# A Fourier layer and a feed-forward layer on one core: where the feed-forward's streamed operands lie, relative to its weights, modulo 512 bytes

## The chip, the core and the metric

The kernel runs on one core of a Trainium2 chip. The core has a matrix engine (PE, TensorE), whose matmuls take a *stationary* operand (the weights, loaded into the array by an own weight-load instruction, PEld) and a *moving* operand (streamed past them column by column), two elementwise engines that also read the matrix engine's result memory (DVE, ACT), a slower one that does not (POOL), and SP, which here only issues transfers (DMA). Operands of matmuls are read from the on-chip memory SBUF, in which each of 128 partitions has its own row of bytes; a tile's *place* below is its byte address in that row. The metric is device microseconds of one execution.

## The reference

```python
X = np.fft.rfft(x, axis=1)                      # x: 8 batches x 3008 x 256
Yr = Xr @ w_r - Xi @ w_i + b_r
Yi = Xr @ w_i + Xi @ w_r + b_i
Y = softshrink(Yr, 0.01) + 1j * softshrink(Yi, 0.01)
y = np.fft.irfft(Y, n=3008, axis=1)             # 24064 tokens of 256
h = y @ w_in                                    # 256 x 2048
out = (h * np.cos(h)) @ w_out                   # 2048 x 256
```

## The kernel before

The Fourier part is done as small matrix products in stages: stage A (along 47, line 364), stage B (forward along 64 at line 396, the mixing products at lines 420 to 422, the inverse along 64 at line 460), stage C (the last inverse, line 715), with scratch in DRAM between them. The feed-forward part works on tiles of 512 tokens (the sixth and last of a batch has 448) and on 16 slices of 128 of the 2048 hidden units. Each operand that needs more than the fast format holds is split into a high and a low part; one step of the feed-forward (`moe_step`, one tile and one slice) therefore issues six matmuls into `ph` (lines 772, 773, 774, twice: high weights by high tokens, high by low, low by high), then ACT and DVE form `h*cos(h)`, and three steps later `second` issues six matmuls into `po` (lines 742, 743 and 748, twice). Twelve matmuls a step, 96 steps a batch: 1152 a batch, of which 960 have 512 columns and 192 have 448.

The order is written by hand: the feed-forward of batch b runs on PE, and between its matmuls (`pull`) pieces of the Fourier stages of batches b+1 and b+2 are put in by a budget. Batch 7 has no such work beside it but its own stage C. Before the feed-forward of batch 0 there is a prologue of some 96 us with the Fourier stages of batch 0 and part of batch 1's.

What the change touches:

- `tokens` allocates the two tiles `xTh` and `xTl` (moving operands of lines 772 to 774), three buffers each; `moe_step` allocates `gh` and `gl` (moving operands of lines 742, 743 and 748), four buffers each. The stationary operands are 128-column (512-byte) slices of `win` (lines 772 to 774) and `wout` (742 to 748).
- Every one of those tiles is a whole number of 512 bytes long, and in the program built from the kernel `win`, `wout`, `wf`, the `wk` pool and the `mo` pool (all Fourier work tiles, `xTh`, `xTl`, `gh`, `gl`) begin at 320 modulo 512. So each feed-forward matmul has moving operand and weights at a distance of 0 modulo 512. The tiles `fa`, `fas`, `ident` and `inv`, which come ahead of `last` (1128 bytes) and `sig` (48 bytes), begin at 128 modulo 512; `inv` is the stationary operand of line 460 and `fas` that of line 364, whose moving operands (`yh`, `yl`, `xh`) begin at 320. Those two lines are at a distance of 192.
- `AO_BUFS`, the buffers of `stage_out` (tag `ao`): results of stage A (lines 326 and 366) and of the inverse of stage B (lines 463, 530 and 537), copied from the result memory by ACT and then stored to DRAM by SP's queue. The tag `xl` holds `wq`, scratch of the weight splitting (line 216).

Of the kernel before, what the change touches and what calls it, by code (L numbers as in the profile page):

```python
# [12 lines left out]
F32 = mybir.dt.float32  # L13
F32R = mybir.dt.float32r
# [13 lines left out]
NTT = 6  # L28
SKEW = 3
XP_BUFS = 5  # L30
XT_BUFS, AO_BUFS, XH_BUFS = 5, 4, 3
EARLY_W = 6
TAIL_W = 2
W_ORDER = (0, 1, 2, 3, 8, 9, 10, 11, 4, 5, 12, 6, 7, 13, 14, 15)
# [6 lines left out]
GAP = 5  # L41
A_EVERY, A_DVE = 2, 4
NP = 12
SPREAD, SPREAD_FIRST = 1.2, 1.1


# [6 lines left out]
def _split(a):  # L53
    hi = _r11(a)
    return hi, _r11(a - hi.astype(np.float64))
# [7 lines left out]
def _constants():  # L63
# [39 lines left out]
    inv = inv.reshape(2, 128, 2, 32, 2).transpose(1, 0, 3, 2, 4).reshape(128, 2, 128)  # L103
    sg = sign.reshape(64, NP, 2).transpose(2, 0, 1).reshape(128, NP)
    fh, fl = _split(fa.reshape(2, 48, -1)[0, :, :96].reshape(48, 48, 2)[:, :, 0])
# [8 lines left out]
def tile_body(ctx: ExitStack, tc, x, x2, w_r, w_i, b_r, b_i, w_in, w_out,  # L114
# [4 lines left out]
    cp = ctx.enter_context(tc.tile_pool(name="cp", bufs=1))  # L119
    wk = ctx.enter_context(tc.tile_pool(name="wk", bufs=2))  # L120
    pool = {}
    dr = ctx.enter_context(tc.tile_pool(name="dr", bufs=2, space=bass.MemoryType.DRAM))
    ps = ctx.enter_context(tc.tile_pool(name="ps", bufs=1, space=PS))

    fa = cp.tile([96, 128], F32, name="fa")
    nc.sync.dma_start(fa, c_fa)
    fas = cp.tile([112, 128], F32R, name="fas")
    ident = cp.tile([128, 128], F32, name="ident")
    inv = cp.tile([128, 2, 2, 128], F32R, name="inv")
    last = cp.tile([120, 2, 141], F32, name="last")  # L130
    sig = cp.tile([128, NP], F32, name="sig")
    bias = cp.tile([128, 2, 256], F32, name="bias")

    def load_bias():
# [15 lines left out]
    def rest(lo, x, hi):  # L150
        return nc.vector.tensor_tensor(out=lo, in0=x, in1=hi.bitcast(F32), op=ALU.subtract)  # L151
# [25 lines left out]
    def split_f64(k):  # L177

        hi, lo, _ = piece(W_ORDER[k])
        pair = raws[k].rearrange("p (n t) -> p n t", t=2)  # L180
        v, ve = pair[:, :, 1], nc.vector
        first = k < EARLY_W + TAIL_W
        m = wk.tile([128, 512], F32, tag="xh", name="wm", bufs=XH_BUFS)
        tag, bufs = (("fb", 2) if k < EARLY_W + 1 else ("z", 2)) if EARLY_W - 1 <= k and first else ("xh", XH_BUFS)

        def rest_of_words():
            low = wk.tile([128, 512], F32, tag=tag, name="wl", bufs=bufs)
            nc.scalar.activation(low, pair[:, :, 0], AF.Copy, scale=2.0 ** -52)
            return low

        def clip(engine, c):
            engine.tensor_scalar(out=c, in0=m, scalar1=F64_TINY, scalar2=F64_HUGE, op0=ALU.max, op1=ALU.min)
            return c

        def bits(c):
            ve.tensor_scalar(out=au, in0=c.bitcast(U32), scalar1=0x07FFFFFF, scalar2=3,
                             op0=ALU.bitwise_and, op1=ALU.logical_shift_left)
            ve.scalar_tensor_tensor(out=au, in0=v, scalar=0xC0000000, in1=au,
                                    op0=ALU.bitwise_and, op1=ALU.bitwise_or)

        nc.scalar.activation(m, v.bitcast(F32), AF.Abs)
        low = rest_of_words() if not first or tag != "xh" else None
        yield
        if first:
            c = clip(nc.gpsimd, m)
            yield
        bank = f"o{k % 2}" if first else "f"
        a = ps.tile([128, 512], F32, tag=bank, name="wa", bufs=1 if first else 3)
        au = a.bitcast(U32)
        bits(c if first else clip(ve, a))  # L210
        yield
        nc.scalar.copy(hi, a)
        if low is None:
            low = rest_of_words()
        yield
        q = wk.tile([128, 512], F32, tag="xl", name="wq", bufs=XH_BUFS)
        r = wk.tile([128, 512], F32, tag="cl" if k == EARLY_W + TAIL_W - 1 else "wa", name="wr", bufs=1)
        ve.tensor_scalar(out=q.bitcast(U32), in0=au, scalar1=0xFF800000, scalar2=None, op0=ALU.bitwise_and)
        rest(r, a, hi)
        yield  # L220
        nc.gpsimd.tensor_tensor(out=q, in0=low, in1=q, op=ALU.mult)
        mark["words"] = nc.gpsimd.tensor_tensor(out=lo, in0=r, in1=q, op=ALU.add)

    def piece(k):
        if k < 8:
            q, c = divmod(k, 2)
            cs = slice(512 * q, 512 * q + 512)
            return win[:, 0, c, cs], win[:, 1, c, cs], w_in[128 * c:128 * c + 128, 1024 * q:1024 * q + 1024]
        f = 2 * (k - 8)
        return tuple(wo[0][:, h, f:f + 2].rearrange("p f e -> p (f e)") for h in range(2)) + (  # L230
            w_out[128 * f:128 * f + 256, :].rearrange("(f p) e -> p f e", p=128),)
# [7 lines left out]
    def moe_w():  # L239
        for k in range(EARLY_W + TAIL_W, 16):  # L240
            steps = split_f64(k)
            with tc.issue_after(mark["gh"].ins):
                next(steps)
            yield
            for i, _ in enumerate(steps):
                if i == 0:
                    load_piece()
                yield
            yield
# [121 lines left out]
    def stage_b(b):  # L371
# [4 lines left out]
        def load(m):  # L376
            if m >= NP:
                return
            if m % 2 == 0:
                fb[m // 2] = wk.tile([128, 4, 128], F32, tag="fb", name="fb", bufs=2)  # L380
                with tc.issue_after(mark["words"].ins) if b == 1 and m < 4 else ExitStack():
                    nc.gpsimd.dma_start(fb[m // 2], c_fb[:, 2 * m:2 * m + 4])
            at[m] = stage_in("at")
            nc.sync.dma_start(at[m].rearrange("p (k d) -> p k d", k=2),
                              scr1[b][2 * m:2 * m + 2].rearrange("k r n d -> (r n) k d"))
# [83 lines left out]
        yield 2.5  # L469
        for m in range(NP + 2):  # L470
            if m < NP:
                load(m + 2)
                yield from fwd(m)
            if 1 <= m <= NP:
                yield from wmix(m - 1)
# [4 lines left out]
    def stage_b0():  # L480
# [75 lines left out]
        def words(k):  # L556

            if 0 <= k < EARLY_W + TAIL_W:
                if k not in w:
                    w[k] = split_f64(k)  # L560
                next(w[k], None)
# [119 lines left out]

    xT = {}

    def tokens(b, t):
        if (b, t) not in xT:
            xT[b, t] = tuple(pool["mo"].tile([128, 2, 512], F32R, tag=n, name=n, bufs=3) for n in ("xTh", "xTl"))
        return xT[b, t]

    def stage_c(b, t):
# [75 lines left out]
    def moe_step(b, t, f, pull):  # L765
        th, tl = xT[b, t]
        n = 512 if t < NTT - 1 else 448
        ph = ps.tile([128, 512], F32, tag="h", name="ph", bufs=3)
        h = ph[:, :n]
        fs = slice(128 * f, 128 * f + 128)  # L770
        for c in range(2):
            mm(h, win[:, 0, c, fs], th[:, c, :n], start=c == 0, stop=False)  # L772
            mm(h, win[:, 0, c, fs], tl[:, c, :n], start=False, stop=False)  # L773
            mark["ph"] = mm(h, win[:, 1, c, fs], th[:, c, :n], start=False, stop=c == 1)  # L774
        u = pool["mo"].tile([128, 512], F32, tag="u", name="u", bufs=4)
        k = u.bitcast(I32)
        gh = pool["mo"].tile([128, 512], F32R, tag="gh", name="gh", bufs=SKEW + 1)
        gl = pool["mo"].tile([128, 512], F32R, tag="gl", name="gl", bufs=SKEW + 1)
        nc.scalar.activation(k[:, :n], h, AF.Identity, bias=0.25, scale=1.0 / TWO_PI)  # L779
        nc.vector.scalar_tensor_tensor(out=u[:, :n], in0=h, scalar=1.0 / TWO_PI, in1=k[:, :n],  # L780
                                       op0=ALU.mult, op1=ALU.subtract)
        nc.scalar.activation(u[:, :n], u[:, :n], AF.Sin, bias=HALF_PI, scale=TWO_PI)  # L782
        nc.vector.tensor_tensor(out=u[:, :n], in0=h, in1=u[:, :n], op=ALU.mult)  # L783
        mark["gh"] = nc.scalar.copy(gh[:, :n], u[:, :n])  # L784
        (rest_pool if b == 0 and t < 3 and f < 8 or f % 4 in POOL_GL else rest)(gl[:, :n], u[:, :n], gh[:, :n])
        pend.append((b, t, f, gh, gl))
        pull()
        if len(pend) > SKEW:
            second(*pend.pop(0))
        pull()  # L790
# [3 lines left out]
    with tc.manual_schedule(), ExitStack() as first:  # L794
# [4 lines left out]
        p = ps.tile([128, 512], F32, tag="o0", name="pz", bufs=1)  # L799
# [59 lines left out]
    for b in range(NB):  # L859
        fa = ahead(b)  # L860
        for i, (t, lo, hi) in enumerate(phases(b)):
# [6 lines left out]
            def pull():  # L868
                budget[0] += rate
                while open_[0] and budget[0] > 0:  # L870
                    c = next(fa, None)
                    if c is None:
                        open_[0] = False
                    else:
                        budget[0] -= c
# [9 lines left out]
            while open_[0]:  # L885
                c = next(fa, None)
# [34 lines left out]
```

## Time and profile before

| | |
|---|---|
| time, median of 2 runs (2629.76 to 2630.74) | 2630.25 us |
| span of the profiled execution, first to last instruction | 2628.1 us |
| PE busy | 2619.1 us, 100% |
| PEld, DVE, ACT, POOL busy | 85%, 73%, 71%, 41% |
| PE's share of the chain that ended last | 99% |

The profile is of one execution, whose span is 2628.1 us; the median of the two timed runs is 2.15 us above it, which lies around the span. Ends of matmuls are modelled in the profile, so a matmul's recorded duration is longer than the time until the next one starts (they are pipelined). What a matmul costs is the difference of the start times of two that follow each other, called its *step* here; the timeline gives start times to 0.01 us.

### The profile page before, as it was taken

How to read it: one execution, taken by the hardware profiler on the slowest of the kernel's cores; microseconds unless marked ns; L12 is line 12 of the kernel's file. 1: busy time of each engine (PE TensorE's matmuls, PEld its weight loads, DVE VectorE, ACT ScalarE, POOL GpSimd, SP SyncE). 2: the span in 40 equal slices, each digit the busy share in tenths (PEclk: the TensorE clock that was granted, in tenths of full speed). 3: DMA queues.
4: the chain of work that ended last, by engine and by line, in shares of the span. 5: the costliest groups of instructions: out<-in, count | busy, mean ns of one | idle time of the engine just before them, and what ended most of it. 6: DMA issues, size and time to landing. Idle time of an engine off the chain costs nothing.

```text
span 2628.1 us, 38433 instructions
## 1 busy us (share of the span) xinstructions
PE 2619.1 (100%) x13180; PEld 2241.4 (85%) x13180; DVE 1919.9 (73%) x3237; ACT 1877.5 (71%) x3557; POOL 1085.5 (41%) x916
## 2 busy tenths in 40 slices
PE   9999999999999999999999999999999999999999
PEld 8788888888888888888888888888888888888888
DVE  6888876877677776777767777677776666766665
ACT  5787766777677776777767777677776666666666
POOL 5774543544334443344523444234442333322222
PEclk9999999999999999999999999999999999999999
DMA  7533312322112221123212232123221111010000
GB/s 211 175 95 98 105 59 79 94 88 89 55 60 94 85 86 57 61 93 96 77 56 62 91 96 74 55 62 103 89 71 53 45 54 43 25 53 24 9 17 16
DMA packets 126372, 194.26 MB, mean 74 GB/s; under 512 B 14130, under 2 KB 63618, under 8 KB 126176
## 3 DMA queue, kind: packets, MB, share of 16 engines
q1 hardware_dynamic: 120160, 171.94, 21.0%
q0 software_dynamic: 6016, 19.86, 2.4%
q8 instruction: 104, 1.70, 0.3%
q14 instruction: 92, 0.75, 0.1%
HBM read 119.92 MB, written 71.83 MB: 73 GB/s over the span
## 4 chain that ended last, share of the span: by engine, by line
PE 99%; DVE 0%; DMA 0%; issue 0%; ACT 0%; SPq 0%; ACTq 0%
PE po L742 13%; PE po L743 13%; PE ph L773 13%; PE ph L772 13%; PE po L748 13%; PE ph L774 13%; PE pc L715 4%; PE pb L396 3%; PE p L422 2%; PE p L421 2%; PE p L420 2%; PE pi L460 2%; PE pa L364 2%; PE p L520 1%; PE pa L323 1%; PE pa L297 0%
## 5 line engine op out<-in xcount | busy, mean ns | idle before, releaser
L148 POOL TENSOR_TENSOR gl<-u,gh 128x512 fp32r<-128x512 f32 (+1 forms) x396 | 507.8, 1283 | 958.8 <-ACT gh L784 774.4
L783 DVE TENSOR_TENSOR u<-ph,u 128x512 f32<-128x512 f32 (+1 forms) x768 | 521.0, 679 | 273.0 <-ACT u L782 255.6
L780 DVE SCALAR_TENSOR_TENSOR u<-ph,u 128x512 f32<-128x512 f32 (+1 forms) x768 | 519.5, 677 | 253.4 <-ACT u L779 244.4
L779 ACT ACTIVATE u<-ph 128x512 int32<-128x512 f32 (+1 forms) x768 | 450.2, 587 | 257.1 <-PE ph L774 246.1
L782 ACT ACTIVATE u<-u 128x512 f32<-128x512 f32 (+1 forms) x768 | 479.4, 625 | 201.6 <-DVE u L780 198.7
L772 PE MATMUL ph<-xTh,win 128*128 128x512 f32 (+1 forms) x1536 | 610.4, 398 | 1.4 <-DVE u L783 1.1
L742 PE MATMUL po<-gh,wout 128*128 128x512 f32 (+1 forms) x1536 | 598.2, 389 | 0.0
L773 PE MATMUL ph<-xTl,win 128*128 128x512 f32 (+1 forms) x1536 | 595.0, 387 | 0.0
L743 PE MATMUL po<-gh,wout 128*128 128x512 f32 (+1 forms) x1536 | 594.9, 387 | 0.0
L774 PE MATMUL ph<-xTh,win 128*128 128x512 f32 (+1 forms) x1536 | 594.8, 387 | 0.0
L784 ACT CAST gh<-u 128x512 fp32r<-128x512 f32 (+1 forms) x768 | 467.2, 609 | 134.5 <-DVE u L783 132.6
L748 PE MATMUL po<-gl,wout 128*128 128x512 f32 (+1 forms) x1534 | 476.4, 388 | 0.0
L774 PEld LDWEIGHTS ph<-xTh,win 128*128 128x128 f32 x1536 | 288.7, 188 | 53.8
L742 PEld LDWEIGHTS po<-gh,wout 128*128 128x128 f32 x1536 | 289.1, 188 | 51.7 <-ACT part L754 0.3
L743 PEld LDWEIGHTS po<-gh,wout 128*128 128x128 f32 x1536 | 288.9, 188 | 51.7
L772 PEld LDWEIGHTS ph<-xTh,win 128*128 128x128 f32 x1536 | 289.0, 188 | 49.5 <-DVE u L783 2.0
L748 PEld LDWEIGHTS po<-gl,wout 128*128 128x128 f32 x1534 | 285.5, 188 | 52.2
L773 PEld LDWEIGHTS ph<-xTl,win 128*128 128x128 f32 x1536 | 289.5, 188 | 46.5
L151 DVE TENSOR_TENSOR gl<-u,gh 128x512 fp32r<-128x512 f32 (+1 forms) x372 | 273.6, 736 | 50.0 <-ACT gh L784 43.0
L148 POOL TENSOR_TENSOR xh<-xt,xh 48x512 fp32r<-48x512 f32 x144 | 188.5, 1310 | 204.4 <-ACT xh L352 194.3
L446 POOL TENSOR_TENSOR z<-z,cl 128x512 f32<-128x512 f32 x84 | 110.0, 1310 | 208.9 <-DVE cl L445 198.0
L367 DVE TENSOR_TENSOR ao<-pa,ao 48x512 f32<-48x512 f32 x192 | 133.0, 693 | 22.7 <-ACT ao L366 17.4
(122 smaller groups left out, 3110.7 us busy)
## 6 DMA issues: line engine op xcount, KB each, us to landing
xt<-in_dram SPq DMA_DIRECT2D x192, 224.0 KB, 2.6
scr<-bo SPq DMA_DIRECT2D x95, 256.0 KB, 2.0
bt<-scr SPq DMA_DIRECT2D x96, 240.0 KB, 3.1
at<-scr SPq DMA_DIRECT2D x84, 256.0 KB, 2.7
out_dram<-ob SPq DMA_DIRECT2D x80, 256.0 KB, 2.3
scr<-ao SPq DMA_DIRECT2D x192, 96.0 KB, 1.9
fb<-in_dram POOLq DMA_DIRECT2D x46, 256.0 KB, 3.2
raw<-in_dram POOLq DMA_DIRECT2D x14, 512.0 KB, 4.4
```

The lines of the kernel that those rows point to most:

```text
L148: return nc.gpsimd.tensor_tensor(out=lo, in0=x, in1=hi.bitcast(F32), op=ALU.subtract)
L742: mm(po[e][:, :n], wo[0][:, 0, f, es], gh[:, :n], start=f == first, stop=False)
L743: mm(po[e][:, :n], wo[0][:, 1, f, es], gh[:, :n], start=False, stop=False)
L748: mm(po[e][:, :n], wo[0][:, 0, f, es], gl[:, :n], start=False, stop=f == last_f)
L772: mm(h, win[:, 0, c, fs], th[:, c, :n], start=c == 0, stop=False)
L773: mm(h, win[:, 0, c, fs], tl[:, c, :n], start=False, stop=False)
L774: mark["ph"] = mm(h, win[:, 1, c, fs], th[:, c, :n], start=False, stop=c == 1)
L779: nc.scalar.activation(k[:, :n], h, AF.Identity, bias=0.25, scale=1.0 / TWO_PI)
L780: nc.vector.scalar_tensor_tensor(out=u[:, :n], in0=h, scalar=1.0 / TWO_PI, in1=k[:, :n], op0=ALU.mult, op1=ALU.subtract)
L782: nc.scalar.activation(u[:, :n], u[:, :n], AF.Sin, bias=HALF_PI, scale=TWO_PI)
L783: nc.vector.tensor_tensor(out=u[:, :n], in0=h, in1=u[:, :n], op=ALU.mult)
L784: mark["gh"] = nc.scalar.copy(gh[:, :n], u[:, :n])
```

## The change

Batches are numbered 0 to 7, as in the code. `xTh` and `xTl` become the two halves of one tile `xT`, and `gh` and `gl` those of one tile `g`. Each of these tiles is 512 bytes longer than its contents, and the contents begin `SHIFT[b]` floats into it: 0, 16, 32, 64, 128, 256, 384 and 192 bytes in batches 0 to 7. `sig` and `last` are allocated first, so that `fa`, `fas`, `ident` and `inv` come to lie at 320 modulo 512 as well, and everything from `bias` on stays where it was modulo 512. To make room, `AO_BUFS` goes from 4 to 3 and `wq` from 3 buffers to 2.

```diff
-XT_BUFS, AO_BUFS, XH_BUFS = 5, 4, 3
+XT_BUFS, AO_BUFS, XH_BUFS = 5, 3, 3
...
+SHIFT = (0, 4, 8, 16, 32, 64, 96, 48)
...
+    sig = cp.tile([128, NP], F32, name="sig")
+    last = cp.tile([120, 2, 141], F32, name="last")
     fa = cp.tile([96, 128], F32, name="fa")
...
-    last = cp.tile([120, 2, 141], F32, name="last")
-    sig = cp.tile([128, NP], F32, name="sig")
...
-        q = wk.tile([128, 512], F32, tag="xl", name="wq", bufs=XH_BUFS)
+        q = wk.tile([128, 512], F32, tag="xl", name="wq", bufs=2)
...
+    def shifted(b, name, size, bufs):
+        return pool["mo"].tile([128, size + 128], F32R, tag=name, name=name, bufs=bufs)[:, SHIFT[b]:SHIFT[b] + size]
+
     def tokens(b, t):
         if (b, t) not in xT:
-            xT[b, t] = tuple(pool["mo"].tile([128, 2, 512], F32R, tag=n, name=n, bufs=3) for n in ("xTh", "xTl"))
+            both = shifted(b, "xT", 2048, 3)
+            xT[b, t] = tuple(both[:, v:v + 1024].rearrange("p (c n) -> p c n", c=2) for v in (0, 1024))
...
-        gh = pool["mo"].tile([128, 512], F32R, tag="gh", name="gh", bufs=SKEW + 1)
-        gl = pool["mo"].tile([128, 512], F32R, tag="gl", name="gl", bufs=SKEW + 1)
+        both = shifted(b, "g", 1024, SKEW + 1)
+        gh, gl = both[:, :512], both[:, 512:]
```

On PE every instruction keeps its place in the order, and none waits for another engine than before; only the names of the streamed tiles differ. A piece of PE's order in the first feed-forward tile of batch 0, as it was:

```order
L772 MATMUL ph<-xTh,win 128x512
L773 MATMUL ph<-xTl,win 128x512
L774 MATMUL ph<-xTh,win 128x512
L748 MATMUL po_1135<-gl,wout 128x512
L748 MATMUL po_1136<-gl,wout 128x512
```

The same five of the changed program (its line numbers are five higher here):

```order
L777 MATMUL ph<-xT,win 128x512
L778 MATMUL ph<-xT,win 128x512
L779 MATMUL ph<-xT,win 128x512
L753 MATMUL po_1129<-g,wout 128x512
L753 MATMUL po_1130<-g,wout 128x512
```

Nothing moved: the same kinds in the same order read tiles that lie elsewhere. On ACT the copies into `ao` and `bo` wait for other stores than before, since a buffer comes round after three uses and not four. At the end of the prologue, with the semaphores that each waits for in brackets (DMAHW ones are of stores), before:

```order
L326 COPY ao<-pa 96x512 [waits DMAHW3_49,PE_49,Activation_49]
L530 COPY bo<-pi 128x512 [waits DMAHW4_49,PE_49,Activation_49]
L326 COPY ao<-pa 96x512 [waits DMAHW0_49,PE_49,Activation_49]
L537 COPY bo<-pi 128x256 [waits DMAHW1_49,PE_49]
L326 COPY ao<-pa 96x512 [waits PE_49]
L537 COPY bo<-pi 128x256 [waits DMAHW4_49,PE_49,Activation_49]
L201 ACTIVATE wm<-raw 128x512 [waits DMASW5_49,Pool_49]
```

And in the changed program:

```order
L327 COPY ao<-pa 96x512 [waits DMAHW4_49,PE_49,Activation_49]
L531 COPY bo<-pi 128x512 [waits DMAHW0_49,PE_49,Activation_49]
L327 COPY ao<-pa 96x512 [waits DMAHW1_49,PE_49,Activation_49]
L538 COPY bo<-pi 128x256 [waits DMAHW4_49,PE_49]
L327 COPY ao<-pa 96x512 [waits PE_49]
L538 COPY bo<-pi 128x256 [waits DMAHW5_49,PE_49,Activation_49]
L202 ACTIVATE wm<-raw 128x512 [waits DMASW5_49,Pool_49]
```

The order is the same; the first of the two half copies (line 537, now 538) waits for the store that had been the second one's to wait for, which is the store of the first row here.

## Rows read from the trace of the kernel before

**Rows 1.** The page: busy time, PE's granted clock, and the chain that ended last.

```profile
PE 2619.1 (100%) x13180; PEld 2241.4 (85%) x13180; DVE 1919.9 (73%) x3237; ACT 1877.5 (71%) x3557; POOL 1085.5 (41%) x916
...
PEclk9999999999999999999999999999999999999999
...
PE 99%; DVE 0%; DMA 0%; issue 0%; ACT 0%; SPq 0%; ACTq 0%
```

**Rows 2.** The longest wait of PE: total us, times, longest us.

```profile
PE pz L801 <- DVE idle L797: 1.5, 1, 1.5
```

**Rows 3.** Stretches of batches 0, 2, 5, 7: us, then PE, PEld, DVE, ACT, POOL.

```profile
96.67:419.34 322.67, 321.54 (x1632) 275.97 (x1632) 266.91 (x442) 245.23 (x476) 179.77 (x152) 1.00 0.31 94
743.43:1067.37 323.94, 323.94 (x1643) 278.45 (x1641) 240.30 (x406) 238.41 (x455) 135.76 (x115) 1.00 0.25 77
...
1715.23:2039.16 323.93, 323.93 (x1642) 278.45 (x1641) 240.45 (x406) 238.43 (x455) 135.76 (x115) 1.00 0.25 77
2355.08:2623.56 268.48, 268.48 (x1238) 227.62 (x1237) 164.96 (x256) 175.82 (x315) 62.08 (x49) 1.00 0.05 16
```

**Rows 4.** Timeline of PE in batch 3 (start us, us): 256 columns, then 512.

```profile
1192.21 0.28 PE L420 MATMUL p<-wf,Xh 128*128 128x256 f32 x1
...
1192.92 0.40 PE L742 MATMUL po<-gh,wout 128*128 128x512 f32 x1
...
1194.31 0.39 PE L772 MATMUL ph<-xTh,win 128*128 128x512 f32 x1
...
1197.03 0.39 PE L772 MATMUL ph<-xTh,win 128*128 128x512 f32 x1
1197.26 0.63 PE L460 MATMUL pi<-yh,inv 128*128 128x512 f32 x2
1197.72 0.40 PE L460 MATMUL pi<-yl,inv 128*128 128x512 f32 x1
1197.96 0.40 PE L364 MATMUL pa<-xh,fas 112*128 112x512 f32 x1
1198.20 0.40 PE L773 MATMUL ph<-xTl,win 128*128 128x512 f32 x1
```

**Rows 5.** Timeline of PE in batch 7, last tile (448 columns).

```profile
2600.66 0.36 PE L772 MATMUL ph<-xTh,win 128*128 128x448 f32 x1
...
2605.53 0.36 PE L772 MATMUL ph<-xTh,win 128*128 128x448 f32 x1
```

**Rows 6.** PE's groups by shape, stretch of batch 3: count | busy us, mean ns.

```profile
L743 PE MATMUL po<-gh,wout 128*128 128x512 f32 x160 | 62.7, 392 | 0.0
...
L364 PE MATMUL pa<-xh,fas 112*128 112x512 f32 x32 | 12.9, 402 | 0.0
...
L460 PE MATMUL pi<-yh,inv 128*128 128x512 f32 x22 | 6.9, 395 | 0.0
L460 PE MATMUL pi<-yl,inv 128*128 128x512 f32 x11 | 4.4, 397 | 0.0
```

**Rows 7.** One of the same groups in the stretch of batch 7.

```profile
L743 PE MATMUL po<-gh,wout 128*128 128x512 f32 x160 | 62.3, 389 | 0.0
```

**Rows 8.** Timeline of ACT and SP at the prologue's end, and store landing times.

```profile
83.56 0.58 ACT L326 COPY ao<-pa 96x512 f32<-96x512 f32 x1 [1.31 <-issue]
84.17 0.31 SPq L331 DMA_DIRECT2D scr<-ao  x1
...
85.80 0.37 ACT L537 COPY bo<-pi 128x256 f32<-128x256 f32 x1
...
scr<-ao SPq DMA_DIRECT2D x16, 192.0 KB, 3.9
```

**Rows 9.** The closest reuse of `ao` in the feed-forward, and its stores' landing.

```profile
197.64 0.95 SPq L368 DMA_DIRECT2D scr<-ao  x2
...
200.41 0.58 ACT L366 COPY ao<-pa 48x512 f32<-48x512 f32 x1
...
scr<-ao SPq DMA_DIRECT2D x192, 96.0 KB, 1.9
```

## The prediction

> **What bounds the kernel now.** I read the page first. PE is busy for 100% of the span and is 99% of the chain that ended last, at the full granted clock from end to end, which is the 2.4 GHz level [rows 1]. PE's longest wait in the whole run is 1.5 us [rows 2]. So PE hardly waits for anybody, and the time is the sum of PE's steps. DVE and ACT are busy for 240 and 238 us of a batch's 324 us, POOL for 136 [rows 3]: what is made slower there has some 80 us a batch to hide in. A term of this change must therefore be either a longer or shorter PE step, or a new wait long enough to reach PE.
>
> The second thing to see is how exactly it repeats. Batches 2 to 5 are four in a row, the first of 323.94 us and the last of 323.93 [rows 3]; a batch is its own measuring instrument, good to 0.01 us.
>
> The third is the steps themselves, from start to start. Twelve feed-forward matmuls of 512 columns from 1194.31 to 1197.03 take 2.72 us, 226.7 ns each [rows 4]. In 512 columns at 2.4 GHz there are 213.3 ns, so 13 ns of each step are something else. Six matmuls of 256 columns take 0.71 us, 118 ns each [rows 4]; from 118 to 226.7 is 0.425 ns a column, which leaves 9 to 10 ns that belong to the matmul and not to its columns, once for each weight load.
>
> The fourth is what happens where the distance is not 0. Right behind that even stretch come three of line 460 and one of line 364, at a distance of 192 bytes: 1197.26 to 1198.20, 0.94 us for four, 235 ns each [rows 4]. The first pair takes 0.46 us, the third and the fourth 0.24 each [rows 4]: about 233 for the three. All have 512 columns, and no wait stands in these rows. The recorded durations say the same over a batch: 395 and 397 ns for line 460 and 402 for line 364, against 392 for the feed-forward's line 743 of the same width [rows 6]. And line 743 itself is at 389 in batch 7, where lines 460 and 364 never come between, against 392 in batch 3 [rows 6, 7]. So 226.7 is an undisturbed step, 226.7 + 2.5 (from the 3 of the rounded means) = 229.2 is the mean in a batch with other work in it, and a matmul at a distance of 192 takes some 233 to 235.
>
> **The change, part by part.** *Order.* PE's sequence and the engines it waits for stay; no instruction is added on any engine that does work. What is left is where operands lie, and buffers.
>
> *Fewer buffers.* Once the feed-forward runs, the closest case is the copy at 200.41, which with three buffers needs the first of two stores issued at 197.64: 2.77 us for a store that lands 1.9 us after its issue [rows 9]. That holds, and nothing is queued behind. At the prologue's end it doesn't: the half copy at 85.80 comes to need the store issued at 84.17, and such stores take 3.9 us to land (median), so to 88.1 [rows 8]. ACT's queue then waits up to 2.3 us; behind it stand the weight splits and the first token copies, which PE needs for its first feed-forward matmul. Bounds 0 and 2.3 us; I take +1, since ACT has short gaps later in which it catches up. The second `wq` buffer less is of the same kind, on POOL in the same stretch; it is inside these bounds.
>
> *Merged tiles.* With `gh` and `gl` in one buffer the next `gh` waits until the last `gl` matmul of four steps earlier is done. PE issues that matmul a whole step ahead of the `ph` matmuls from which the new `gh` is formed, so nothing is late. Price 0; without that cover it would be one matmul, 0.2 us a step.
>
> *Lines 460 and 364 go to a distance of 0.* In the whole run 33 × 7 = 231 of line 460 at 512 columns and 32 × 6 = 192 of line 364 (counts of one batch in [rows 6]). If their steps become 226.7, each gains 8.3 at most: 423 × 8.3 = −3.5 us. In batch 0, whose feed-forward distance stays 0, part of the disturbance behind them goes too: 2.5 ns × 960 = 2.4 us at most, and the switches between 256 and 512 columns and to fp32 stay, so −1. Together −4.5.
>
> *Batch 7, distance 192.* This is the one distance that the trace has at 512 columns. I take 233.3, the mean of the three of line 460: 960 × (233.3 − 226.7) = +6.3 us. At 448 columns a step is 4.87 / 24 = 202.9 [rows 5]; the trace has no other distance at that width; bounds 0 and +6.6 ns × 192 = 1.3 us; I take +0.4.
>
> *Batches 1 to 6, distances 16, 32, 64, 128, 256 and 384.* Unknown. The nearest rows are the two distances that the trace has, 226.7 (0) and 233.3 (192), and I take the middle, 230.0, being equally far from both: 960 × (230.0 − 229.2) = 0.8 us a batch, +4.6 in six. Ends: all six at 226.7, undisturbed, −14.4 us; all six at 233.3, +23.6. The price can be outside too, down to 217 (no cost per matmul: 512 × 0.425) or up, and the rivals have that. The 448-column tiles I leave at their time.
>
> *DVE, ACT and POOL* write and read the shifted tiles. If a shifted operand cost them 5%, it would be 12 of the 80 us they have free in a batch.
>
> Sum: 1.0 − 4.5 + 6.3 + 0.4 + 4.6 = +7.8 us on the span of 2628.1, so 2635.9; with the 2.15 us that the median of the runs lies above the span, **2638 us**. That is within 2%, which is about what a measurement of this kernel can tell from no change.
>
> **A rule against it.** In rows, neighbouring matmuls of one width differ by 233 to 235 against 226.7 where the distance does [rows 4]. The Trainium skill (TensorE: Matmul & The Clock Gate, Part 2, step 1) says that PE has two independent SBUF read ports and that loading the next weights takes nothing from the running matmul's reads. By that rule a distance could cost nothing, and only the buffers would be left, so 2630 to 2632. The trace speaks against it, by 7 ns a matmul, but for two lines only, and those differ from the feed-forward in more than the distance (line 364 has 112 rows, both write another result bank).
>
> **Rivals.**
>
> 1. *The place plays no part.* Lines 460 and 364 are slow because of their rows, their result bank or the change of line, and all that happens is the buffers' 0 to 2.3 us: 2630 to 2633. For it: the two confounders just named, and that the step at 460 is not one number (0.46 for two, then 0.24). Against: line 460 reads 128 rows as the feed-forward does. This is also the case that the change doesn't do what it says. Chance 0.15.
>
> 2. *Most distances are as good as 0* (a shorter period than 512, or any constant distance settles at 226.7). Then the disturbances go too: −14.4 − 4.5 + 1 and 0 to 6 for batch 7: 2612 to 2619. For it: undisturbed stretches settle at exactly one value. Against: 192 does not. Chance 0.13.
>
> 3. *Every distance but 0 is as bad as 192 or a little worse*: 233.3 in seven batches, +23.6 + 6.3, and up to 1.3 us a batch at 448 columns: 1 − 4.5 + 29.9 + (0 to 9), so 2657 to 2666. For it: a disturbed batch is slower than an undisturbed one, as if 0 were a special place. Chance 0.16.
>
> 4. *Slower by over 2%, the other side*: a streamed row that begins 16 or 32 bytes into what was a whole stretch, or collides with the weight load from end to end, costs a second time what a weight load costs now (10 ns or more). It decides from 52.6 us / (7 × 1152) = 6.5 ns a matmul on average over all seven shifted batches, so about 235.5 at 512 columns; all seven at 240 would be 960 × (6 × 10.8 + 13.3) = 75 us more: 2705. For it: 235 and 402 ns durations exist [rows 4, 6]. Against: no stretch of the trace stays there. Chance 0.04.
>
> 5. *Faster by over 2%*: most distances are free of the 9 to 10 ns. At 217 in all seven, 960 × (6 × 12.2 + 9.7) = 80 us less: 2546. It decides at about −6.5 ns on average, 222.5. For it: nothing says that 0 is the best place, only that it is better than 192. Against: no 512-column stretch of the trace runs under 226. Chance 0.03.
>
> **How the numbers follow.** The forecast, a mean of 228 to 232 for the six unknown distances (which moves the sum by −11.5 and +11.5 us: 2627 to 2650), has 0.49; with rivals 1 to 3 that is 0.93 for within 2%. Faster 0.03, slower 0.04. The range leaves out rivals 4 and 5 and the outer edges of 2 and 3: 2614 to 2663. The likeliest one's own range is 2627 to 2650.
>
> **What would show it.** The length of each batch's stretch in the changed trace: batch 0 (from its first line 772) shorter by 1 to 2 us than its 322.7 [rows 3]; batch 7 longer than 268.5 by some 6 us; batches 2 to 5 no longer alike, each showing its own distance. In the timeline, even stretches in each batch: 226.7 in batch 0, about 233 in batch 7. Lines 460 and 364 at about 389 ns of recorded duration, not 395 to 402, at least in batch 0. If batch 7 keeps 268.5 the confounders were the cause and the forecast rests on nothing; if any batch is under 310, there is a better place than 0; if PE shows a wait over 2 us, it is a buffer and not a place. The first matmul of line 772 later than 96.67, where batch 0's stretch begins [rows 3], by over 2.3 us would mean that I undercounted the buffers.

## The result, and the profile after

The changed kernel takes **2649.91 us** (2649.54 to 2650.29, 2 runs) against 2630.25: a ratio of 1.0072, interval 1.0056 to 1.0089. It is slower by 19.7 us, clear of noise, inside the range, and within the 2% that were called no change; the point, 2638, was 12 us short.

PE's row on the page, against [rows 1]:

```profile
PE 2639.0 (100%) x13180; PEld 2243.6 (85%) x13180; DVE 1919.5 (72%) x3237; ACT 1879.4 (71%) x3557; POOL 1087.5 (41%) x916
...
PEclk9999999999999999999999999999999999999999
```

PE gained 19.9 us of busy time with the same number of instructions; the other engines stayed within 2.2 us. The stretches of the eight batches (us, PE busy, count of matmuls; then clock, DMA share, GB/s), which answer to [rows 3]:

```profile
97.93:419.99 322.06, 320.87 (x1632) 1.00 0.31 94
419.99:746.40 326.41, 326.41 (x1644) 1.00 0.25 77
746.40:1074.08 327.68, 327.68 (x1643) 1.00 0.25 76
1074.08:1399.37 325.29, 325.29 (x1643) 1.00 0.25 77
1399.37:1726.37 327.00, 327.00 (x1642) 1.00 0.25 76
1726.37:2050.27 323.90, 323.90 (x1643) 1.00 0.25 77
2050.27:2369.60 319.33, 319.33 (x1610) 1.00 0.14 43
2369.60:2643.94 274.34, 274.34 (x1239) 1.00 0.04 15
```

Batches 2 to 5, alike to 0.01 us before, now differ from each other by up to 3.8 us. Batch 5, at 256 bytes, is where it was (323.90, before 323.93). Batch 7, at 192, grew from 268.48 by 5.86 us. The even step of batch 7, which answers to the 226.7 ns of [rows 4], from its timeline (start us, us):

```profile
2450.87 0.39 PE L777 MATMUL ph<-xT,win 128*128 128x512 f32 x1
...
2452.27 0.39 PE L747 MATMUL po<-g,wout 128*128 128x512 f32 x1
```

Six steps in 1.40 us: 233.3 ns each. Lines 460 and 364 (now 461 and 365) in batch 5, where all distances are whole multiples of 256, which answer to [rows 6]:

```profile
L365 PE MATMUL pa<-xh,fas 112*128 112x512 f32 x32 | 12.8, 401 | 0.0
...
L461 PE MATMUL pi<-yh,inv 128*128 128x512 f32 x22 | 6.8, 389 | 0.0
L461 PE MATMUL pi<-yl,inv 128*128 128x512 f32 x11 | 4.3, 389 | 0.0
```

Line 460 came down from 395 and 397 to 389 ns, line 364 hardly at all, from 402 to 401. So the prediction's two lines did not behave alike.

The end of the prologue, against [rows 8]: the two half copies on ACT, and the first matmul of stage C on PE (the bracket is the idle time before it and what ended it):

```profile
86.81 0.37 ACT L538 COPY bo<-pi 128x256 f32<-128x256 f32 x1 [0.48 <-DMA scr<-ao]
...
87.88 0.37 ACT L538 COPY bo<-pi 128x256 f32<-128x256 f32 x1 [0.17 <-DMA scr<-bo]
...
94.38 3.23 PE L720 MATMUL pc<-last,bt 120*128 120x141 f32 x24 [1.57 <-DMA bt<-scr]
```

ACT waited for stores where three buffers said it would, 0.65 us in all; later PE waited 1.57 us for the load of a stage C operand from the scratch in DRAM, and the feed-forward began 1.26 us later than before. That the first led to the second is not shown: in run 3 below ACT waits as long, and the feed-forward begins only 0.15 us later than before.

### The profile page after: what moved, and what is told of

It is laid out like the page before. It is cut to its first block, busy times and chain, and to the rows that moved or that the text cites. A ratio compares the mean times of both kernels' runs of the same rounds, so it can differ in the third digit from the quotient of the medians.

```text
span 2648.5 us, 38448 instructions
## 1 busy us (share of the span) xinstructions
PE 2639.0 (100%) x13180; PEld 2243.6 (85%) x13180; DVE 1919.5 (72%) x3237; ACT 1879.4 (71%) x3557; POOL 1087.5 (41%) x916
## 4 chain that ended last, share of the span: by engine, by line
PE 99%; DVE 0%; DMA 0%; issue 0%; ACT 0%; ACTq 0%
PE ph L777 13%; PE po L747 13%; PE ph L779 13%; PE ph L778 13%; PE po L753 13%; PE po L748 13%; PE pc L720 4%; PE pb L397 3%; PE p L423 2%; PE p L422 2%; PE p L421 2%; PE pi L461 2%; PE pa L365 2%; PE p L521 1%; PE pa L298 1%; PE pa L324 0%
## 5 line engine op out<-in xcount | busy, mean ns | idle before, releaser
L149 POOL TENSOR_TENSOR g<-u,g 128x512 fp32r<-128x512 f32 (+1 forms) x396 | 509.7, 1288 | 970.5 <-ACT g L789 763.6
L787 ACT ACTIVATE u<-u 128x512 f32<-128x512 f32 (+1 forms) x768 | 479.6, 625 | 200.4 <-DVE u L785 197.6
L777 PE MATMUL ph<-xT,win 128*128 128x512 f32 (+1 forms) x1536 | 613.8, 400 | 1.5 <-DVE u L788 1.2
L747 PE MATMUL po<-g,wout 128*128 128x512 f32 (+1 forms) x1536 | 601.8, 392 | 0.0
L779 PE MATMUL ph<-xT,win 128*128 128x512 f32 (+1 forms) x1536 | 598.4, 390 | 0.0
L748 PE MATMUL po<-g,wout 128*128 128x512 f32 (+1 forms) x1536 | 597.2, 389 | 0.0
L778 PE MATMUL ph<-xT,win 128*128 128x512 f32 (+1 forms) x1536 | 597.2, 389 | 0.0
L789 ACT CAST g<-u 128x512 fp32r<-128x512 f32 (+1 forms) x768 | 467.1, 609 | 130.5 <-DVE u L788 128.3
L753 PE MATMUL po<-g,wout 128*128 128x512 f32 (+1 forms) x1534 | 480.4, 391 | 0.0
L779 PEld LDWEIGHTS ph<-xT,win 128*128 128x128 f32 x1536 | 288.8, 188 | 56.7
L747 PEld LDWEIGHTS po<-g,wout 128*128 128x128 f32 x1536 | 289.0, 188 | 54.7 <-ACT part L759 0.3
L748 PEld LDWEIGHTS po<-g,wout 128*128 128x128 f32 x1536 | 289.1, 188 | 54.2
L777 PEld LDWEIGHTS ph<-xT,win 128*128 128x128 f32 x1536 | 289.1, 188 | 51.6 <-DVE u L788 2.0
L753 PEld LDWEIGHTS po<-g,wout 128*128 128x128 f32 x1534 | 285.7, 188 | 54.9
L778 PEld LDWEIGHTS ph<-xT,win 128*128 128x128 f32 x1536 | 289.6, 189 | 48.7
L152 DVE TENSOR_TENSOR g<-u,g 128x512 fp32r<-128x512 f32 (+1 forms) x372 | 273.3, 735 | 49.6 <-ACT g L789 43.6
```

The lines of the kernel that those rows point to most:

```text
L149: return nc.gpsimd.tensor_tensor(out=lo, in0=x, in1=hi.bitcast(F32), op=ALU.subtract)
L747: mm(po[e][:, :n], wo[0][:, 0, f, es], gh[:, :n], start=f == first, stop=False)
L748: mm(po[e][:, :n], wo[0][:, 1, f, es], gh[:, :n], start=False, stop=False)
L753: mm(po[e][:, :n], wo[0][:, 0, f, es], gl[:, :n], start=False, stop=f == last_f)
```

## The experiments

The theory: a feed-forward step on PE is set by the distance between the streamed operand and weights, modulo some power of two. The rivals: the longer, merged tiles or the fewer buffers cost the time; the absolute place does; the place plays no part. Stretches are quoted as above.

**1. The alignment of `fas` and `inv` alone.**

```diff
+    sig = cp.tile([128, NP], F32, name="sig")
+    last = cp.tile([120, 2, 141], F32, name="last")
     fa = cp.tile([96, 128], F32, name="fa")
...
-    last = cp.tile([120, 2, 141], F32, name="last")
-    sig = cp.tile([128, NP], F32, name="sig")
```

> The kernel before with one part of the change alone: sig and last are allocated first, so that fas and inv lie at a distance of 0 from what they are multiplied with; no shift, no merged tiles, all buffers as before. Theory (the distance sets the step): lines 460 and 364 gain up to 8 ns each and disturb less behind them; batch 0 of the changed kernel, which has just this, is 0.6 us shorter, so seven batches 0.6 to 1 us shorter each, batch 7 unchanged at 268.5: 2624 to 2626 us. Rival (place plays no part): 2630.2, batches 2 to 5 at 323.93.

Measured 2629.85 us, ratio 0.9999 (0.9990 to 1.0008): the expected 4 to 6 us are not there. Batches 0, 3 and 7:

```profile
96.59:418.57 321.98, 320.86 (x1632) 1.00 0.31 95
...
1066.56:1390.43 323.87, 323.87 (x1642) 1.00 0.25 77
...
2354.19:2622.83 268.64, 268.64 (x1239) 1.00 0.05 16
```

Batch 0 lost 0.69 us (0.61 in the changed kernel), batch 3 only 0.06, and batch 7 grew by 0.16. In batch 3 the groups by shape say why:

```profile
L364 PE MATMUL pa<-xh,fas 112*128 112x512 f32 x32 | 12.8, 401 | 0.0
...
L460 PE MATMUL pi<-yh,inv 128*128 128x512 f32 x22 | 6.8, 389 | 0.0
```

Line 460's mean step, from the starts in the timeline, went from 234.2 to 226.7 ns: 33 × 7.5 = 0.25 us a batch, so for this line the distance was the cause. Line 364 went from 235.1 to 233.2 (0.06 us) and stays slow at a distance of 0, for another reason. What was won was mostly lost again in the same batch: the 448-column steps went up from 204.0 to 204.5 ns in the mean and took 0.12 us more in all, and the 512-column ones 0.15 us more, nearly all of it in the 32 steps of over 260 ns that stand right behind fp32 matmuls.

**2. The fewer buffers alone.**

```diff
-XT_BUFS, AO_BUFS, XH_BUFS = 5, 4, 3
+XT_BUFS, AO_BUFS, XH_BUFS = 5, 3, 3
...
-        q = wk.tile([128, 512], F32, tag="xl", name="wq", bufs=XH_BUFS)
+        q = wk.tile([128, 512], F32, tag="xl", name="wq", bufs=2)
```

> The kernel before with the other small part alone: AO_BUFS 3 and wq 2. Theory: the feed-forward begins 1.3 us later (at 97.9 instead of 96.67), as in the changed kernel, and every batch keeps its length: 2631.5 us. Rival: the buffers also cost something in batches 1 to 6, whose sum grew by 13.9 us: any batch longer than before by over 0.1 us would say so.

Measured 2630.92 us, ratio 1.0003 (0.9993 to 1.0012). The feed-forward begins at 97.18, 0.5 us later and not 1.3; the batches are what they were:

```profile
97.18:419.89 322.71, 321.59 (x1631) 1.00 0.31 94
...
1067.92:1391.86 323.94, 323.94 (x1643) 1.00 0.25 77
...
2355.64:2624.12 268.48, 268.48 (x1238) 1.00 0.05 16
```

So no batch owes its length to buffers. The beginning varies from one program to the next by more than this effect: with the very same prologue code it was 97.93 in the changed kernel, 96.82 in run 3, 98.14 and 97.07 in runs 5 and 6, and 99.79 in run 9. In run 3 ACT waits at its half copies as it does in the changed kernel (0.64 us against 0.65), and yet PE waits only 0.23 us for the load where it waited 1.57 there:

```profile
86.95 0.37 ACT L538 COPY bo<-pi 128x256 f32<-128x256 f32 x1 [0.46 <-DMA scr<-ao]
...
88.04 0.37 ACT L538 COPY bo<-pi 128x256 f32<-128x256 f32 x1 [0.18 <-DMA scr<-bo]
...
93.20 3.30 PE L720 MATMUL pc<-last,bt 120*128 120x141 f32 x24 [0.23 <-DMA bt<-scr]
```

So the 1.26 us of the changed kernel are not the price of ACT's waits alone; what else sets that load's landing is open.

**3. One distance, 256 bytes, in all batches.**

```diff
-SHIFT = (0, 4, 8, 16, 32, 64, 96, 48)
+SHIFT = (64,) * 8
```

> The changed kernel with 256 bytes as the shift of every batch. Theory (distance with a period of 256 bytes): all batches as with a distance of 0: batch 7 back at 268.5 +- 0.2, batches 2 to 5 at 323.9 or up to 1 us less, so 2626 to 2632 us. Rival (batch 5 is as fast as before for another reason, for instance the buffers that its tiles fall on): batches 1 to 4, 6 and 7 stay 1 to 6 us longer than before, 2645 or more.

Measured 2630.44 us, ratio 0.9999 (0.9990 to 1.0009). Batches 0, 3 and 7:

```profile
96.82:418.91 322.09, 320.91 (x1631) 1.00 0.31 94
...
1066.90:1390.78 323.88, 323.88 (x1643) 1.00 0.25 77
...
2354.54:2623.18 268.64, 268.64 (x1239) 1.00 0.05 16
```

Every batch is within 0.11 us of run 1, which has a distance of 0: 256 bytes are as good as none. The merged and lengthened tiles, which this kernel has, cost nothing that these batches show.

**4. The distance of 192 everywhere, without the change's code.**

```diff
     wo = [cp.tile([128, 2, NFC, 256], F32R, name="wout")]
+    cp.tile([128, 48], F32, name="pad")
```

> The kernel before with 192 empty bytes behind wout (and wq with 2 buffers, to make room): the streamed tiles and all Fourier work tiles move up by 192 bytes, win, wout and wf stay, no tile is merged or lengthened. Theory (distance): batch 7 as in the changed kernel, 274.3 us, the other batches 3 to 5 us longer than before each, 2655 to 2670 us. Rival (the longer, merged tiles of the changed kernel cost the time, not the distance): 2630 to 2632, batch 7 at 268.5.

Measured 2659.87 us, ratio 1.0109 (1.0092 to 1.0126). Batches 3 and 7:

```profile
1078.10:1405.28 327.18, 327.18 (x1643) 1.00 0.24 76
...
2379.55:2653.96 274.41, 274.41 (x1238) 1.00 0.04 15
```

Batch 7 has the 274.3 of the changed kernel to 0.1 us, from 192 empty bytes and one `wq` buffer less (run 2: no batch changed). The rival of the merged tiles is out.

**5 and 6. Sixteen other distances.** The changed kernel with

```diff
-SHIFT = (0, 4, 8, 16, 32, 64, 96, 48)
+SHIFT = (12, 20, 24, 28, 36, 40, 44, 52)
```

> The changed kernel with eight other distances: 48, 80, 96, 112, 144, 160, 176 and 208 bytes in batches 0 to 7. Theory (distance modulo 256, 0 the only place where the even step at 512 columns is 226.7): every batch longer than in the kernel with 256 bytes everywhere (322.1, 324.1, 323.9 four times, 316.0, 268.6), by 1 to 6 us, with even steps of 228 to 236 ns at 512 columns; 2645 to 2660 us in all. Rival (some distance is better than 0): a batch shorter than there by over 1 us, with an even step under 226.

and with

```diff
-SHIFT = (0, 4, 8, 16, 32, 64, 96, 48)
+SHIFT = (56, 60, 68, 1, 2, 3, 62, 63)
```

> The changed kernel with 224, 240, 272, 4, 8, 12, 248 and 252 bytes in batches 0 to 7. Theory with a period of 256 bytes: batch 2 (272) has the steps that 16 bytes had in the changed kernel, about 231.7 ns at 512 columns and 200 to 202 at 448. If memory is read in whole lines of 16 bytes or more, and the even place is a whole one, then 4, 8 and 12 bytes either act as 0 (about 323.9 us a batch) or as 16 (326.4); if it goes by single words, they lie between. Rival: the smallest distance makes the largest difference, over 327.

Measured 2661.67 and 2658.42 us, one time each. From run 6, batches 2 to 5, with 272, 4, 8 and 12 bytes:

```profile
752.90:1078.88 325.98, 325.98 (x1643) 1.00 0.25 76
1078.88:1410.79 331.91, 331.91 (x1642) 1.00 0.25 75
1410.79:1739.39 328.60, 328.60 (x1643) 1.00 0.25 76
1739.39:2062.97 323.58, 323.58 (x1642) 1.00 0.25 77
```

All of it in one table: the batch's length less that of the same batch in run 3, and the mean feed-forward steps from the starts in the timeline. Only steps under 260 ns are taken; that leaves out those right behind a group of fp32 matmuls, whose last record is short (in batch 3 of the kernel before mostly 26 to 31 ns, and the next step mostly 314 to 329).

| bytes (batch, run) | longer by, us | 512 columns, ns | 448 columns, ns |
|---|---|---|---|
| 0 (0, changed kernel) | −0.03 | 228.0 | 203.3 |
| 4 (3, run 6) | 8.03 | 237.0 | 206.5 |
| 8 (4, run 6) | 4.73 | 233.4 | 206.5 |
| 12 (5, run 6) | −0.29 | 229.4 | 200.6 |
| 16 (1, changed kernel) | 2.29 | 231.7 | 201.7 |
| 32 (2, changed kernel) | 3.81 | 233.2 | 203.3 |
| 48 (0, run 5) | 3.88 | 232.6 | 202.9 |
| 64 (3, changed kernel) | 1.41 | 231.1 | 200.8 |
| 80 (1, run 5) | 1.97 | 231.3 | 203.7 |
| 96 (2, run 5) | 4.24 | 233.3 | 205.1 |
| 112 (3, run 5) | 2.60 | 231.4 | 206.2 |
| 128 (4, changed kernel) | 3.13 | 232.4 | 203.7 |
| 144 (4, run 5) | 3.73 | 232.8 | 206.2 |
| 160 (5, run 5) | 4.07 | 233.7 | 202.5 |
| 176 (6, run 5) | 3.74 | 232.6 | 203.9 |
| 192 (7, changed kernel) | 5.70 | 233.3 | 202.3 |
| 208 (7, run 5) | 6.59 | 233.9 | 203.9 |
| 224 (0, run 6) | 4.54 | 233.2 | 203.8 |
| 240 (1, run 6) | 5.08 | 234.6 | 203.1 |
| 248 (6, run 6) | 3.06 | 232.5 | 200.9 |
| 252 (7, run 6) | 1.38 | 229.0 | 200.8 |
| 256 (5, changed kernel) | 0.03 | 229.0 | 204.6 |
| 272 (2, run 6) | 2.11 | 231.6 | 201.5 |
| 384 (6, changed kernel) | 3.31 | 232.3 | 203.7 |

Each distance was tried in one batch, and the batches differ in the other work between their matmuls: the same 192 bytes make batch 7 longer by 5.8 us and batch 3 by 3.3 (run 4 against run 3), though their steps are alike, 233.3 and 233.2 ns. So rows of different batches are better compared by their steps than by the first column.

256 acts as 0, 272 as 16 (231.6 and 231.7 ns), 384 nearly as 128. No distance is better than 0 at 512 columns; the rival of a better place falls there. At 448 columns seven are 1.8 to 3.8 ns better than 0 is in the same batch of run 3 (12, 16, 64, 160, 248, 252 and 272; there it is 204.5 in batches 1 to 5, 204.2 in batch 6 and 202.6 in batch 7), and 12 bytes make a batch shorter as a whole. My expectation for the words of a line (4, 8 and 12 bytes act as 0, as 16, or lie between) fails in all its forms, and its rival holds: 4 bytes are the worst of all, 8 come next among the small ones, 12 are nearly as good as 0.

**7. Own weights or the next ones?** The changed kernel without shifts, but with `wout` and `g` both 192 bytes on:

```diff
+    cp.tile([128, 48], F32, name="pad1")
     wo = [cp.tile([128, 2, NFC, 256], F32R, name="wout")]
+    cp.tile([128, 80], F32, name="pad2")
...
     def shifted(b, name, size, bufs):
+        off = 48 if name == "g" else 0
-        return pool["mo"].tile([128, size + 128], F32R, tag=name, name=name, bufs=bufs)[:, SHIFT[b]:SHIFT[b] + size]
+        return pool["mo"].tile([128, size + 128], F32R, tag=name, name=name, bufs=bufs)[:, off:off + size]
```

> The kernel before's distances split in two: win and xT lie at 320 modulo 512, wout and g both 192 bytes further. Each matmul still has its own operands at a distance of 0; only where a matmul on one pair runs while the weights of the other are loaded (2 of 12 in a feed-forward step) the streamed operand and the weights being loaded are 64 or 192 apart. Theory A (the distance to the matmul's own weights counts): batch 7 at 268.6 us. Theory B (the distance to the weights that are loaded while it runs, those of the next matmul, counts): two disturbances in each step of twelve, which each take three to five matmuls to settle, so 3 to 5 ns a matmul more: batch 7 at 272 to 274.

Measured 2640.09 us, one time. Batches 5 and 7:

```profile
1720.27:2044.93 324.66, 324.66 (x1642) 1.00 0.25 77
...
2362.10:2633.75 271.65, 271.65 (x1239) 1.00 0.04 16
```

Batch 7 is 3.0 us above run 3, its mean step 230.3 ns, though every matmul lies right to its own weights. Theory A, 268.6, is out. B had 272 to 274, so its size was a little too large, but it is the one of the two that foresaw a loss. It is not shown alone, though: twice in twelve matmuls the streamed operands, and the weights, also change their own places by 192 bytes here, and no run separates that from the distance to the weights being loaded. Nor do the single steps point at one matmul. The timeline has the load of the next weights begin together with each matmul; the sixth into `ph` and the sixth into `po`, beside which the other side's weights are loaded, take 231.0 and 226.0 ns (means of batch 7), and the longest are the third and fourth into `ph` (232.9 and 234.6) and the second into `po` (235.1).

**8. Everything 192 bytes further up.**

```diff
+    cp.tile([128, 48], F32, name="pad")
     fa = cp.tile([96, 128], F32, name="fa")
```

> The kernel before with 192 empty bytes ahead of everything (and wq with 2 buffers): all places move by 192, all distances stay. Theory (distance): batches 2 to 5 at 323.93, batch 7 at 268.48, 2630 to 2631 us. Rival (the absolute place of the streamed operands counts, which moved in the same way in the kernel with 192 bytes behind wout): 2655 to 2660, batch 7 at 274.

Measured 2629.97 us, ratio 0.9999 (0.9988 to 1.0011):

```profile
1066.97:1390.90 323.93, 323.93 (x1642) 1.00 0.25 77
...
2354.69:2623.17 268.48, 268.48 (x1239) 1.00 0.05 16
```

Each batch as before to 0.02 us. Moving all places by 192 bytes changes nothing; so it is not the absolute place that made run 4 slower.

**9 and 10. What the scan is worth.** Distance 0 at 512 columns, and for the sixth tile of each batch another one:

```diff
+LAST = 3
...
+    def shifted(t, name, size, bufs):
+        off = LAST if t == NTT - 1 else 0
+        return pool["mo"].tile([128, size + 128], F32R, tag=name, name=name, bufs=bufs)[:, off:off + size]
```

> The changed kernel with a distance of 0 for the five tiles of 512 columns of every batch, and of 12 bytes for the sixth, of 448. Theory (the distance sets the even step, and the best one is another at 448 columns): the 448-column mean falls from 204.5 to some 200.7 ns, as it was with 12 bytes in batch 5 of the second scan, 192 x 3.8 = 0.7 us a batch in batches 1 to 5, 0.4 to 0.6 in the others; batch 7 at 268.1, batches 2 to 5 at 323.2; 2624 to 2626 us in all. Rival (going from one distance to another disturbs the tiles of 512 columns, or the 448-column gain was due to a batch's own conditions): no gain, 2629 to 2632.

Measured 2624.93 us, ratio 0.9980 (0.9971 to 0.9989): 5.4 us less than the kernel before, 2630.29 in the same series. That is clear of noise, if far under 2%. Batches 3 and 7:

```profile
1067.75:1390.85 323.10, 323.10 (x1642) 1.00 0.26 77
...
2352.40:2620.60 268.20, 268.20 (x1239) 1.00 0.05 16
```

The 448-column mean is 200.4 or 200.5 ns in every batch, 4.1 below run 3's 204.5 in batches 2 to 5, and the 512-column mean there is unchanged at 229.0. The other variant takes `LAST = 16` and moves `wf`:

```diff
-LAST = 3
+LAST = 16
...
+    cp.tile([128, 16], F32, name="pad1")
     wf = cp.tile([128, 3, 2, 2, 256], F32R, name="wf")
+    cp.tile([128, 112], F32, name="pad2")
```

> The same with 64 bytes for the sixth tile in place of 12, and with the mixing weights wf moved 64 bytes up, so that lines 420 to 422 (256 columns, stationary Xh and Xl) have a distance of 64 instead of 0. In the kernel with 192 bytes behind wout, where these lines had 64, their mean step was 117.9 ns against 119.3: 216 x 1.4 = 0.3 us a batch in batches 1 to 5, 2 us in all, so 2622 to 2624 us. Rival: they only hand the difference on to the matmuls behind them, whose disturbance begins from another place: the mean step of the feed-forward at 512 columns rises above 229.05 and the total stays at that of the kernel with 12 bytes.

Measured 2624.22 us, ratio 0.9975 (0.9965 to 0.9985):

```profile
1065.14:1388.16 323.02, 323.02 (x1643) 1.00 0.25 77
```

64 bytes do what 12 do. The mixing products went from 119.3 to 118.6 ns, half of what was expected, and the lines behind them gave part of it back (line 460 from 226.7 to 227.6, the feed-forward from 229.04 to 229.10): 0.08 us a batch in batches 2 to 5 and not 0.3 (only batch 1 gained 0.35). That is nearly the rival's case; the intervals of the two kernels overlap.

## Why the prediction was right, and where it was short

**What bounds the kernel** held: from the first feed-forward matmul on PE was busy all the time in every run but for about 1 us in batch 0, the batches differed by its steps alone, and DVE, ACT and POOL hid whatever shifted operands cost them.

**Batch 7** was the best of the terms: +6.7 forecast (6.3 and 0.4), +5.86 measured, with the even 233.3 ns that three matmuls of line 460 had shown. A 448-column step became 0.3 ns shorter there, where 2 ns longer was forecast.

**Batches 1 to 6** were the term that was mis-sized: +4.6 forecast, 14.0 measured against run 3 (2.29 + 3.81 + 1.41 + 3.13 + 0.03 + 3.31). The step that failed is "I take the middle, 230.0, being equally far from both". The six came to 231.7, 233.2, 231.1, 232.4, 229.0 and 232.3, a mean of 231.6, with 256 near the good end and the other five all above the middle. Of the 23 distances other than 0 in the table, only 12, 252 and 256 are below 231 in the mean. A place that one finds even and exact, next to one that is not, is more likely the exception than one end of a scale; rival 3 had that thought, though 256 bytes speak against its "every distance". The time, 2649.91, lies at the upper edge of the forecast's own range (2627 to 2650) and below rival 3's 2657.

**Lines 460 and 364 at distance 0**, −4.5: the step that failed hardest. The batches of run 1 sum to −0.65. For line 460 the reading was right; line 364 is slow for some other reason. Of the confounders that I had named, another result bank holds for line 460 too, which did come down; the 112 rows are line 364's alone, but no run tries them. And a matmul's gain isn't simply added: in batch 3 of run 1, 0.30 us won at the two lines left 0.06. Batch 0 became 0.61 us shorter in the changed kernel, not 1 to 2.

**The buffers**, +1: in the changed kernel's profile +1.26, ACT waiting in the very place, but 0.65 us where the bound was 2.3, and what PE waited for was a load from DRAM, not the weight splits. Run 2 has +0.5, run 3 +0.15 with the same waits of ACT, and the five kernels with the same prologue spread over 3 us. So the size is not settled, and that the profile's +1.26 came near +1 is luck.

Together 1.26 − 0.65 + 14.0 + 5.7 = 20.3 us, against 20.4 between the spans. The buffers, batch 7 and the merged tiles (0, run 3) were right to 1 us; the other two terms missed by 9 and 4 us in the same direction. That the time still fell inside the range owes to the range's width, not to those two terms.

**Rivals.** Rival 1, that the place plays no part, fell with runs 3 and 4: with 192 bytes everywhere the kernel took 29.5 us longer, with 256 everywhere no longer than before. The Trainium skill (TensorE: Matmul & The Clock Gate, Part 2, step 1) says that loading the next tile's weights takes no read bandwidth from the running matmul. What the prediction drew from it, that a distance could cost nothing, does not agree with run 4. That the two reads get in each other's way in the memory is the simplest reading of runs 3, 4, 7 and 8, but no trace shows it: the weight loads have the same recorded 188 ns in the changed kernel as in the kernel before (mean ns of one before the second bar; first the row before, then the row after):

```profile
L743 PEld LDWEIGHTS po<-gh,wout 128*128 128x128 f32 x1536 | 288.9, 188 | 51.7
...
L748 PEld LDWEIGHTS po<-g,wout 128*128 128x128 f32 x1536 | 289.1, 188 | 54.2
```

Rival 2, a shorter period, was right about the period (256 and not 512) and wrong about what lies inside it. The 235.5 ns from which rival 4 decides were passed by 4 bytes alone (237.0, a distance that the change does not have), rival 5's 222.5 by none. (Rival 5's sum is off: 80 us less than 2630 are 2550, not 2546.)

## What to carry to other kernels

Where PE is busy all the time, look at the step from start to start against columns divided by the clock; if some nanoseconds a matmul are left, the distance between the streamed operand and the weights is a free parameter, and padding of a few bytes moves it. Keep it constant, so that the steps settle, and scan it for each width by giving each repetition of the program its own value, with a run at one constant value to compare each repetition with: one run here tried eight distances, where an unchanged batch repeats to some hundredths of a microsecond. Between two known values of such a parameter don't interpolate.

## What was not expected of the hardware

- Undisturbed stretches often settle at the same mean steps: 200.0 and 206.7 ns at 448 columns, 226.7 and 233.3 at 512 (as the six steps of batch 7 above). All four are whole multiples of 6.67 ns (30, 31, 34 and 35 times); single steps, such as 231 and 236 by turns in batch 7 of the changed kernel, add up to such multiples (467 = 70 times). It is no rule, though: batch 7 holds about 228.9 ns for long stretches at 252 bytes (run 6) and about 234.6 at 208 (run 5).
- At distance 0 the 448-column tiles have two states: an even 206.7 ns, and a repeating pattern of 199 to 207 ns with a mean of about 202.7. Batch 7 of the kernel before shows only the second, batch 3 stretches of both. What decides between them is open. At 12 and 64 bytes it is 200.0 in the undisturbed stretches of all batches (runs 9 and 10).
- 4 bytes do more harm than any other distance tried: 8.0 us in one batch, 237.0 ns a step, where 12 bytes do none. What order lies in that is open, as is why line 364 takes 232 to 236 ns at every distance tried.
